# Block-sorted attention and a gated MLP on one core: first batch's V by transfers, and a new order of units

## The chip, the cores and the metric

The kernel runs on one core of a Trainium2 chip. The metric is the device time of one execution in microseconds; lower is better. Times of several runs are given as a median with the lowest and the highest.

## The reference

Four batches, eight heads, 768 tokens, head size 64; the tokens of a head stand in 8 blocks of 96. A 8x8 matrix P per head is normalised five times (exponential, rows, columns); K and V are mixed over blocks with it; attention runs inside each block; the result goes through a gated MLP whose gate mixes tokens.

```python
P = sort_net
for _ in range(5):
    P = P - np.max(P, axis=-1, keepdims=True)
    P = np.exp(P)
    P = P / (np.sum(P, axis=-1, keepdims=True) + 1e-09)
    P = P / (np.sum(P, axis=-2, keepdims=True) + 1e-09)
k_sorted = np.einsum('bhij,bhjcd->bhicd', P, k_b)      # the same for v
scores = scale * np.matmul(q_b, k_sb.transpose(0, 1, 2, 4, 3))
attn = softmax(scores)                                  # over the keys of the block
x = np.matmul(attn, v_sb)                               # heads side by side: 768 x 512 per batch
h = np.maximum(x @ w_in, 0.0)                           # 512 -> 1024
u, v = h[..., :512], h[..., 512:]
v_s = np.einsum('ts,bsd->btd', w_spatial, layernorm(v)) + b_spatial[None, :, None]
out = (u * v_s) @ w_out
```

## The kernel before

The work is cut into units, each a few instructions on one or two engines, and `ORDER` is a written-out list of the units in the order in which they are issued. Every engine runs its own instructions in that order and waits where an operand isn't ready, so the list decides what stands behind a wait. A unit is `NAME:arguments`; where the first argument is a digit it is one of four PSUM tiles (`ps0` to `ps3`), and a letter A, D or P says that ScalarE (ACT), VectorE (DVE) or GpSimd (POOL) takes the result out.

Loads: `L:q:b:lo:hi`, `L:k`, `L:v` (heads lo to hi of batch b, cast to bf16 by the transfer, issued by POOL, 768 KB as it lands), `L:wu`, `L:wv` (the halves of w_in, 512 KB), `L:wsa`, `L:wsb` (the halves of w_spatial, 576 KB), `L:wo`, `BI` (the bias). `LH` loads half of the first batch's q uncast by a hardware queue, and `QC` casts it. `S0` loads the sort matrix, `SK:n` is one of the five normalisations (an exponential on ACT, six small operations on DVE), `PR`, `P0`, `PC`, `PD` spread the result into block-mixing matrices `pd`, for batch 0 by DVE and for the others by POOL. `DM` are dummy matmuls that keep TensorE (PE) busy before there is work.

Attention of a batch, by pairs of heads `hp` (0 to 3) and halves of blocks `ih` (0, 1): `QT` turns q on PE (12 transposes, L314), `QQ` does two pairs. `KT` mixes and turns K in one step (12 matmuls, L383, into `kt_all`). `SC` makes scores (8 matmuls, L442) and their exponential on ACT (L447) into one of 5 buffers `ex_all`. `AT` multiplies by V (8 matmuls, L488), and DVE divides by the sums (L495, L496). V must stand with its keys on partitions, as `vb`, one buffer for even and one for odd batches. Batches 1 to 3: `VM` mixes V whole, 2 matmuls of 128x384 for a pair of heads (L410), into `vm`; `VC:b:lo:hi` copies `vm` into `vb` block by block with one 99 KB transfer for each of 8 blocks, issued by SP (L423). Batch 0: `VT` mixes V as K is mixed (12 matmuls, L383) and `VB` turns it back (8 transposes, L401).

The MLP: `XT`, `XX`, `XD` turn the attention's output (on PE by 2 pairs or by 4, or by a transfer), `VP` (one or two of 6 token tiles, L554) and `UP` (L597) are the first layer, `WW` turns w_spatial (L531), `ST`, `LN`, `LA` normalise, `SP` mixes tokens (L609), `GT` multiplies the gate, `OP`, `OE`, `OS` are the last layer with its copies and stores. `SH`, `GH`, `OH`, `OI`, `OJ` do the same for the end of batch 3 in smaller pieces. `QP` and `QX` turn the last batch's q by a transfer. `IV:n` sets the columns of ones in `vb[0]`, `vb[1]` or `vm` (n = 2) on POOL.

Work of several batches is interleaved, and all four batches use the same four PSUM tiles.

Of the kernel before, what the change touches and what calls it, by code (L numbers as in the profile page):

```python
# [28 lines left out]
UP:1:A:0:0:1 LA:0:2 AT:0:1:1:1 LA:0:3 LA:0:1 LA:0:0 SC:2:1:2:1 UP:3:A:0:1:1 AT:0:1:2:1 LA:0:4 VM:1:A:2:0 WW:2:D:0
VM:3:A:2:1 LA:0:5 L:k:3:0:8 SC:0:1:1:0 WW:1:D:2 VM:3:A:2:3 XT:2:D:1:1:0 VM:0:D:2:2 SC:1:1:0:0 AT:3:1:3:0 QQ:2:D:2:2  # L30
AT:0:1:1:0 SP:1:0:1 XT:2:A:1:1:2 AT:3:1:0:0 SP:0:0:3 VC:2:4:8 GT:P:0:3 XT:1:A:1:0:2 XT:2:D:1:0:0 SP:3:0:0 KT:1:A:2:2
KT:0:A:2:0 VC:2:0:4 KT:2:D:2:3 QQ:3:A:2:0 KT:1:A:2:1 SC:2:2:2:1 VP:0:A:1:0:1 GT:D:0:0 QP:A:3:3 ST:1:1 ST:1:0
VP:3:A:1:4:5 ST:1:4 ST:1:5 GT:P:0:1 SC:1:2:0:0 SC:2:2:1:1 SP:0:0:2 SC:3:2:0:1 SC:1:2:3:1 VP:2:A:1:2:3 QP:A:3:1
GT:D:0:2 AT:1:2:0:0 UP:3:A:1:0:1 ST:1:2 AT:0:2:3:1 UP:2:A:1:0:0 ST:1:3 LN:1:0:6 AT:3:2:1:1 LA:1:3 OP:0:0:0:2 OE:A:0:0
LA:1:5 AT:3:2:0:1 VM:1:A:3:2 QP:A:3:2 UP:2:A:1:1:0 QP:D:3:0 LA:1:2 LA:1:1 VM:3:D:3:0 OP:0:0:2:2 QX:3:0:4 LA:1:0
AT:1:2:2:1 OE:A:0:2 KT:3:A:3:1 KT:2:D:3:2 LA:1:4 XD:2:1 SC:1:2:2:0 SC:0:2:1:0 SC:3:2:3:0 OP:2:0:4:2 VM:0:D:3:1
AT:3:2:2:0 SP:1:1:3 OE:A:0:4 AT:0:2:1:0 AT:2:2:3:0 SP:3:1:2 UP:1:A:1:1:1 KT:2:D:3:3 GT:D:1:2 XD:2:0 KT:0:A:3:0
VM:3:A:3:3 VC:3:4:8 SP:1:1:1 SC:2:3:1:1 SC:0:3:2:1 VP:3:D:2:4:5 SC:0:3:3:1 SC:2:3:1:0 ST:2:4 OS:0:4 VP:1:A:2:0:1
# [27 lines left out]
def kernel(  # L66
# [58 lines left out]
    nc.scalar.preload_act_table_set("natural_log_exp_and_others")  # L125
# [104 lines left out]
    def u_SK(n, safe=False):  # L230
# [13 lines left out]
        nc.vector.reduce_sum(out=cols, in_=p_all.rearrange("p i j -> p j i"), axis=AX.X)
# [151 lines left out]
    def u_VB(ps, eng, b, hp):  # L396
        b, hp = int(b), int(hp)
        t = ps_tile(ps, BF16)[0:BLK, 0, :].rearrange("p (i c) -> p i c", i=NB)
        vT = turned("vT", b, hp)
        for i in range(NB):  # L400
            nc.tensor.transpose(t[:, i, :], vT[:, i * BLK:(i + 1) * BLK], ident)  # L401
# [18 lines left out]
    def u_VC(b, lo, hi):  # L420
        b = int(b)
        for i in range(int(lo), int(hi)):
            queue("S").dma_start(  # L423
                out=vb[b % 2][:, i].rearrange("c h d -> c (h d)"),
                in_=vm[i * TB:(i + 1) * TB].rearrange("t g h d -> t g (h d)"),
            )
# [400 lines left out]
```

## Time and profile before

| | us |
|---|---|
| median of 3 runs | 156.18 (155.99 to 156.47) |
| span of the profiled execution, first to last instruction | 154.5 |
| PE busy in it | 146.7 |
| DVE busy | 115.4 |
| ACT busy | 85.5 |
| POOL busy | 39.4 |

The profile gives the profiled execution its span alone; the median of the timed runs is 1.7 us above that span. Starts in the trace count from the start of the span. In a row of a group stand the line, the engine, the operation, the tiles written and read, the shape and the count; then the busy time in us, the mean of one instruction in ns, and the engine's idle time before them. The chain of work is followed back from the last instruction, each piece with its start, its length in us, its engine and line. Rows of transfers give the size and the time from the start of the issue to the landing.

### The profile page before, as it was taken

To read this page: it belongs to the slowest core of one execution; us is meant where nothing else is said; L and a number is where in the kernel's file an instruction comes from. 1 tells how busy PE (TensorE), PEld (TensorE's weight loads), DVE (VectorE), ACT (ScalarE), POOL (GpSimd) and SP (SyncE) were. 2 spreads that over 40 slices of the span, in tenths; PEclk is the share of its full clock that TensorE was granted. 3 is DMA by queue.
4 is the path that set the end of the run, shared out by engine and by line. 5 is a ranking of instruction groups with operands and counts; after the bars stand their busy time and mean duration, and the time that the engine had idled before them with its cause. 6 is when DMAs were issued, how large, how long until landed. Compare 5 with 4: busy or idle time off the path is not lost.

```text
span 154.5 us, 4033 instructions
## 1 busy us (share of the span) xinstructions
PE 146.7 (95%) x1689; PEld 95.7 (62%) x1689; DVE 115.4 (75%) x258; ACT 85.5 (55%) x116; POOL 39.4 (25%) x45
## 2 busy tenths in 40 slices
...
DMA  2999999999999999990069358704708400307756
GB/s 68 270 204 203 204 206 204 209 216 248 223 205 256 205 231 245 208 195 15 4 118 125 67 102 167 182 3 37 205 0 215 163 0 4 132 4 284 268 191 220
DMA packets 30693, 24.36 MB, mean 158 GB/s; under 512 B 10384, under 2 KB 27792, under 8 KB 30672
## 3 DMA queue, kind: packets, MB, share of 16 engines
...
q10 hardware_dynamic: 576, 0.66, 1.2%
...
## 4 chain that ended last, share of the span: by engine, by line
PE 84%; DMA 7%; ACT 2%; DVE 2%; POOL 1%; issue 1%; POOLq 0%; ACTq 0%
PE ps L609 15%; PE ps L554 14%; PE ps L597 14%; PE ps L635 10%; DMA k_in<-in_k_dram 7%; PE ps L442 5%; PE ps L488 5%; PE ps L665 5%; PE ps L383 4%; PE ps L685 3%; PE ps L314 2%; PE ps L410 2%; PE ps L518 2%; ACT ex_all L447 2%; PE ps L531 1%; PE ps L401 1%
## 5 line engine op out<-in xcount | busy, mean ns | idle before, releaser
L626 POOL TENSOR_TENSOR gt<-z,u_sb 128x768 bf16<-128x768 f32 x7 | 11.4, 1640 | 77.0 <-DVE z L615 47.6
L447 ACT ACTIVATE ex_all<-ps 96x768 bf16<-96x768 f32 x32 | 24.7, 806 | 5.7 <-PE ps L442 5.5
L609 PE MATMUL ps<-wspT,v_sb 128*128 128x384 bf16 x144 | 25.1, 326 | 0.0
L597 PE MATMUL ps<-xT,w_in_sb 128*128 128x384 bf16 x128 | 22.8, 326 | 0.0
L496 DVE TENSOR_TENSOR x_sb<-ps,rec_all 96x512 bf16<-96x512 f32 x32 | 22.0, 686 | 1.1
L554 PE MATMUL ps<-w_in_sb,xT 128*128 128x512 bf16 x96 | 22.3, 380 | 0.0
L571 DVE BATCH_NORM_STATS2 stats<-v_sb 128x6 f32<-128x512 bf16 x24 | 16.3, 678 | 4.5 <-ACT v_sb L121 4.5
L115 ACT COPY o_sb<-ps 128x1024 f32<-128x1024 f32 (+1 forms) x12 | 10.9, 905 | 14.6 <-PE ps L685 9.1
L609 PEld LDWEIGHTS <-v_sb 128*128 128x128 bf16 x144 | 13.6, 97 | 8.6
L121 ACT ACTIVATE v_sb<-ps 128x1024 bf16<-128x1024 f32 (+1 forms) x11 | 10.3, 948 | 12.3 <-PE ps L554 12.3
L615 DVE TENSOR_TENSOR z<-ps,b_bc 128x768 f32<-128x768 f32 x12 | 11.4, 954 | 7.3 <-PE ps L609 4.6
L635 PE MATMUL ps<-w_out_sb,gt 128*128 128x256 bf16 x144 | 16.9, 273 | 0.0
L121 ACT ACTIVATE u_sb<-ps 128x768 bf16<-128x768 f32 x12 | 9.7, 811 | 12.7 <-PE ps L597 12.7
L597 PEld LDWEIGHTS <-w_in_sb 128*128 128x128 bf16 x128 | 11.8, 97 | 7.2
L635 PEld LDWEIGHTS <-gt 128*128 128x128 bf16 x144 | 13.8, 97 | 2.1
L554 PEld LDWEIGHTS <-xT 128*128 128x128 bf16 x96 | 8.7, 97 | 9.9
L488 PEld LDWEIGHTS <-ex_all 96*128 96x128 bf16 x256 | 10.7, 97 | 4.0 <-issue 0.5
L488 PE MATMUL ps<-vb,ex_all 96*128 96x65 bf16 x256 | 12.6, 193 | 0.5 <-ACT ex_all L447 0.5
L226 PE MATMUL ps<-warm 128*128 128x512 bf16 x36 | 9.5, 425 | 1.3 <-DVE warm L201 1.3
L442 PE MATMUL ps<-qT,kt_all 64*128 64x96 bf16 x256 | 9.8, 205 | 0.9 <-issue 0.4
L115 ACT CAST kt_all<-ps 128x768 bf16<-128x768 f32 x11 | 8.7, 801 | 2.2 <-PE ps L383 2.2
L442 PEld LDWEIGHTS <-kt_all 64*128 64x128 bf16 x256 | 6.4, 94 | 5.5 <-issue 3.3
...
## 6 DMA issues: line engine op xcount, KB each, us to landing
...
v_in<-in_v_dram POOLq DMA_DIRECT2D x4, 768.0 KB, 21.4
k_in<-in_k_dram POOLq DMA_DIRECT2D x4, 768.0 KB, 23.7
...
q_in<-in_q_dram POOLq DMA_DIRECT2D x3, 768.0 KB, 28.2
...
q<-in_q_dram SPq DMA_DIRECT2D x1, 768.0 KB, 4.6
```

The costliest lines, as they stand in the source:

```text
L115: nc.scalar.copy(out=out, in_=in_)
L121: nc.scalar.activation(out=out, in_=in_, func=AF.Relu)
L442: nc.tensor.matmul(t[:, hh, 0:HW].rearrange("p (g x) -> p g x", g=G)[:, :, ii * TB:(ii + 1) * TB], lhsT=kT[rows, i * BLK:i * BLK + 128], r ...
L447: nc.scalar.activation(out=e_tile(b, hp, ih).rearrange("p h (x g) -> p h x g", g=G), in_=t[0:BLK, :, 0:HW].rearrange("p h (g x) -> p h x g ...
L488: nc.tensor.matmul(t[:, hh, ii * VW:ii * VW + D + 1], lhsT=e[:, c:c + 128], rhs=vb[b % 2][:, ih * NI + ii, 2 * hp + hh, 0:D + 1], start=Tr ...
L496: nc.vector.tensor_mul(out=x_sb[:, hp].rearrange("p i (h d) -> p h i d", h=2), in0=tv[:, :, :, 0:D], in1=_raw_ap(rec, 0, [rec.ap[0], [NI, ...
L554: nc.tensor.matmul(t[:, x, :], lhsT=st["xT", b][:, n // 3, kc, (n % 3) * 128:(n % 3 + 1) * 128], rhs=w_in_sb[:, kc, DH:DFF], start=(kc == ...
L571: nc.vector.bn_stats(out=stats, in_=st["v_sb", b, n])
L597: nc.tensor.matmul(t[:, x, 0:HW], lhsT=w_in_sb[:, kc, mc * 128:(mc + 1) * 128], rhs=st["xT", b][:, ih, kc, :], start=(kc == 0), stop=(kc = ...
L609: nc.tensor.matmul(t[:, x, 0:HW], lhsT=st["v_sb", b, n][:, mc * 128:(mc + 1) * 128], rhs=wspT[:, 3 * x:3 * x + 3, n, :], start=(n == 0), s ...
L615: nc.vector.tensor_add(out=z.rearrange("p (x c) -> p x c", x=2), in0=t[:, :, 0:HW], in1=b_bc.rearrange("p (x c) -> p x c", x=2),)
L635: nc.tensor.matmul(t[:, x, c:c + w], lhsT=st["gt", b, mc][:, (n0 + x) * 128:(n0 + x + 1) * 128], rhs=w_out_sb[:, mc, c:c + w], start=(mc = ...
```

## The change

1. Batch 0's V takes the way of the other batches: four `VM:..:0:..` and `VC:0:..` in place of four `VT` and four `VB`. `VC` gets an argument for the queue, and two of the eight groups of transfers (`VC:0:4:8:0:4:A` and `VC:2:0:4:0:4:A`, four transfers each) are issued by ScalarE.
2. All units have a new order. The loads come as v0, half of q0, k0, q1, v1, k1, wu, wv, wsa, wsb, v2, bias, k2, q2, q3, v3, wo, k3; before, as v0, k0, half of q0, v1, q1, k1, wv, wsb, wu, v2, wsa, q2, bias, k2, q3, wo, v3, k3 (digits are batches).
3. `LH:A` issues the first batch's half of q from ScalarE's queue, ahead of the load of its table (`TB`, which was the first instruction).
4. `SK` writes P a second time by columns (`p_cols`), so that the column sums read neighbours and the two multiplications have the strided side.
5. `vT` gets a zero margin, `vt_all`, and `VB` whole 128-row transposes; neither the new order nor the fall-back path behind `IF` issues a `VT` or a `VB` any more.
6. Several copies change their engine; some store transfers are issued by ScalarE.

```diff
 ORDER = """
-S0 CO SK:0 BH LH:S:0 IV:2 L:v:0:0:8 SK:1 SK:2 ID MA L:k:0:0:8 L:q:0:4:8 DM:3:6:512 DM:0:6:512 L:v:1:0:8 L:q:1:0:8
-QC:A:0 SK:3 QC:A:1 MB SK:4 DM:2:6:512 DM:1:6:512 MC QT:2:D:0:1 DM:1:6:512 DM:3:6:512 PR:1 L:k:1:0:8 QT:2:A:0:0 P0:0:2
-L:wv L:wsb P0:4:6 P0:6:8 IV:0 P0:2:4 PC:D VT:0:A:0:0 KT:3:D:0:0 L:wu PD:1:0:4 VT:2:A:0:1 L:v:2:0:8 KT:1:A:0:3
-KT:0:D:0:2 SC:2:0:0:1 VB:3:D:0:0 PD:1:4:8 KT:1:A:0:1 QT:0:D:0:2 IV:1 QT:2:A:0:3 VB:3:D:0:1 SC:0:0:1:0 VT:1:D:0:3
-VT:2:A:0:2 L:wsa L:q:2:0:8 SC:3:0:0:0 PD:3:0:4 PD:3:4:8 BI AT:0:0:0:1 L:k:2:0:8 VB:1:D:0:3 SC:2:0:1:1 AT:3:0:0:0
-VM:0:A:1:0 VB:1:D:0:2 SC:2:0:2:0 AT:3:0:1:0 SC:0:0:3:0 AT:1:0:2:0 SC:2:0:2:1 AT:3:0:1:1 VM:0:A:1:2 AT:2:0:3:0
-XT:1:A:0:0:0 VM:0:D:1:3 QQ:3:D:1:2 SC:1:0:3:1 VM:2:D:1:1 XT:0:A:0:1:0 KT:1:A:1:2 L:q:3:0:8 AT:3:0:3:1 VC:1:4:8
-KT:0:A:1:1 AT:2:0:2:1 KT:1:A:1:0 VC:1:0:4 QQ:3:D:1:0 KT:0:A:1:3 PD:2:0:4 XT:2:D:0:0:2 XT:1:D:0:1:2 PD:2:4:8 L:wo
-SC:3:1:0:1 SC:0:1:2:0 VP:2:D:0:0:1 ST:0:0 SC:0:1:1:1 SC:1:1:3:1 ST:0:1 VP:3:A:0:4:5 VP:2:A:0:2 VP:1:A:0:3 ST:0:5
+L:v:0:0:8 L:q:0:4:8 S0 LH:A:0 TB CO SK:0 BH ID SK:1 SK:2 MA IV:2 DM:3:6:512 DM:0:6:512 QC:A:0 SK:3 QC:A:1 MB SK:4
+L:k:0:0:8 DM:2:6:512 DM:1:6:512 MC DM:1:6:512 L:q:1:0:8 DM:3:6:512 QT:0:D:0:0 PR:1 P0:0:2 VM:2:A:0:0 P0:2:4 P0:4:6
+P0:6:8 PC:A VM:3:D:0:1 VM:0:A:0:2 VM:2:A:0:3 VC:0:4:8:0:4:A QT:1:D:0:1 PD:1:0:4 QT:3:D:0:2 KT:0:D:0:1 PD:1:4:8
+KT:1:A:0:0 KT:2:D:0:3 L:v:1:0:8 QT:3:D:0:3 KT:0:D:0:2 SC:2:0:1:1 SC:1:0:0:1 L:k:1:0:8 SC:3:0:3:1 QQ:2:D:1:0 QT:0:D:1:2
+QT:1:D:1:3 SC:3:0:2:1 L:wu SC:2:0:1:0 AT:0:0:1:1 VC:0:0:4 SC:1:0:2:0 AT:3:0:0:1 AT:2:0:2:1 SC:0:0:0:0 L:wv VM:1:A:1:1
+L:wsa XT:3:D:0:1:0 PD:2:0:4 AT:0:0:3:1 SC:2:0:3:0 VM:3:A:1:3 AT:1:0:0:0 VM:0:A:1:0 AT:2:0:1:0 VM:3:A:1:2 AT:1:0:3:0
+KT:0:A:1:0 AT:2:0:2:0 KT:3:A:1:2 KT:1:D:1:3 KT:0:A:1:1 XT:2:D:0:1:2 XX:3:D:0:0 SC:1:1:3:1 SC:0:1:1:1 UP:2:A:0:0:1
+SC:3:1:0:1 PD:2:4:8 SC:1:1:2:1 VP:0:A:0:1 VP:2:A:0:0 L:wsb VP:3:A:0:4:3 ST:0:1 VC:1:4:8 AT:1:1:0:1 L:v:2:0:8
+AT:0:1:3:1 BI IV:1 VP:2:D:0:5:2 SC:3:1:3:0 SC:1:1:2:0 UP:0:A:0:1:1 L:k:2:0:8 AT:3:1:1:1 L:q:2:0:8 AT:2:1:2:1 WW:1:A:0
+WW:0:D:2 ST:0:5 UP:3:A:0:1:0 XT:2:D:1:1:2 ST:0:0 L:q:3:0:8 XT:1:A:1:1:0 WW:0:A:4 ST:0:3 SC:3:1:1:0 ST:0:4 ST:0:2
+SC:2:1:0:0 LN:0:0:6 VC:1:0:4 UP:1:A:0:0:0 UP:0:A:1:1:1 VM:3:D:2:0 LA:0:2 UP:2:A:1:0:1 LA:0:1 LA:0:3 LA:0:5 PD:3:4:8
+VM:1:A:2:1 LA:0:4 VP:3:A:1:4 VP:0:A:1:3 LA:0:0 AT:2:1:0:0 KT:1:A:2:1 QQ:3:D:2:2 PD:3:0:4 KT:0:A:2:2 KT:2:D:2:0
+L:v:3:0:8 QQ:1:A:2:0 QP:A:3:2 KT:3:D:2:3 VM:0:A:2:2 QP:D:3:1 SP:2:0:2 AT:3:1:2:0 L:wo AT:1:1:1:0 SP:0:0:0 AT:2:1:3:0
...
-    nc.scalar.preload_act_table_set("natural_log_exp_and_others")
+    def u_TB():
+        nc.scalar.preload_act_table_set("natural_log_exp_and_others")
...
+    p_cols = const.tile([BH, NB, NB], FP32, name="p_cols")
...
-        nc.vector.tensor_mul(out=p_all, in0=p_all, in1=over_rows(rowsum))
-        nc.vector.reduce_sum(out=cols, in_=p_all.rearrange("p i j -> p j i"), axis=AX.X)
+        nc.vector.tensor_mul(out=p_cols.rearrange("p j i -> p i j"), in0=p_all, in1=over_rows(rowsum))
+        nc.vector.reduce_sum(out=cols, in_=p_cols, axis=AX.X)
...
-        nc.vector.tensor_mul(out=to, in0=p_all, in1=over_cols(colsum))
+        nc.vector.tensor_mul(out=to, in0=p_cols.rearrange("p j i -> p i j"), in1=over_cols(colsum))
...
-    def u_VC(b, lo, hi):
-        b = int(b)
+    def u_VC(b, lo, hi, h0=0, h1=HP, eng="S"):
+        b, heads = int(b), slice(2 * int(h0), 2 * int(h1))
         for i in range(int(lo), int(hi)):
-            queue("S").dma_start(
-                out=vb[b % 2][:, i].rearrange("c h d -> c (h d)"),
-                in_=vm[i * TB:(i + 1) * TB].rearrange("t g h d -> t g (h d)"),
+            queue(eng).dma_start(
+                out=vb[b % 2][:, i, heads].rearrange("c h d -> c (h d)"),
+                in_=vm[i * TB:(i + 1) * TB, :, heads].rearrange("t g h d -> t g (h d)"),
             )
```

More of the change, by code (lines that the diff above doesn't have):

```diff
@@ L29 @@
[L29 to L38, printed above, removed]
@@ new lines @@
+VM:3:A:2:3 GT:P:0:0 SP:1:0:3 QP:P:3:3 VC:2:0:4:0:4:A XX:0:D:1:0 SC:3:2:3:0 ST:1:4 SC:2:2:2:1 L:k:3:0:8 VC:2:4:8
+SP:1:0:1 SC:3:2:0:0 SC:0:2:2:0 GT:D:0:2 ST:1:3 VP:2:A:1:2:0 AT:1:2:3:0 GT:P:0:3 GT:P:0:1 QP:D:3:0 AT:3:2:2:1
+VP:0:D:1:1:5 ST:1:2 SC:2:2:0:1 SC:1:2:1:0 OP:3:0:0:2 VM:2:A:3:0 OE:D:0:0 AT:0:2:0:0 UP:1:A:1:1:0 AT:2:2:1:0 AT:3:2:2:0
+ST:1:5 QX:3:0:4 UP:0:A:1:0:0 SC:1:2:3:1 SC:2:2:1:1 OP:3:0:4:2 ST:1:0 ST:1:1 LN:1:0:6 OE:A:0:4 VM:0:D:3:3 LA:1:5
+VM:1:D:3:1 OP:2:0:2:2 LA:1:3 XD:2:0 AT:0:2:0:1 OE:A:0:2 VM:3:A:3:2 VP:1:A:2:1:0 LA:1:0 AT:2:2:1:1 VP:0:D:2:2 OS:0:2
@@ new lines @@
+LA:1:4 LA:1:2 LA:1:1 VC:3:0:4 KT:3:A:3:2 KT:1:A:3:1 KT:2:D:3:3 KT:0:A:3:0 UP:3:D:2:1:0 VC:3:4:8 ST:2:2 SP:1:1:1
+AT:2:2:3:1 SP:0:1:0 SC:3:3:3:0 SC:1:3:1:0 GT:P:1:0 ST:2:1 SP:2:1:2 AT:0:3:3:0 AT:3:3:1:0 XD:2:1 SP:1:1:3 GT:P:1:2
+UP:2:D:2:1:1 ST:2:0 SC:0:3:1:1 SC:3:3:2:0 VP:1:A:2:4 AT:2:3:1:1 GT:D:1:3 VP:0:D:2:3 SC:3:3:3:1 SC:1:3:0:0 UP:2:D:2:0:1
+VP:3:A:2:5 SC:0:3:2:1 ST:2:4 ST:2:5 SC:1:3:0:1 GT:P:1:1 ST:2:3 OP:2:1:2:2 OE:A:1:2 AT:3:3:2:1 AT:0:3:2:0 LN:2:0:6
+LA:2:5 OP:1:1:4:2 LA:2:3 AT:2:3:3:1 LA:2:0 OS:0:0:0:2:A AT:3:3:0:0 LA:2:2 UP:0:A:2:0:0 LA:2:4 LA:2:1 OP:2:1:0:2
@@ L46 @@
+AT:3:3:0:1 XD:3:0 OE:D:1:0 SP:0:2:0 SP:3:2:2 IV:0 GT:P:2:2 OE:A:1:4 OS:1:0:0:2:A SP:1:2:3 XD:3:1 GT:D:2:0 VP:2:D:3:4:5
+SP:0:2:1 ST:3:5 CK VP:3:D:3:2:1 UP:1:A:3:1:0 ST:3:1 VP:2:A:3:3 VP:0:A:3:0 GT:P:2:1 GT:P:2:3 OS:0:4 ST:3:2 ST:3:0
+ST:3:4 OP:1:2:2:2 ST:3:3 CF:2 LF LN:3:0:6 LA:3:5 UP:3:D:3:0:0 OP:0:2:0:2 LA:3:0 LA:3:4 OE:A:2:0 OE:D:2:2 OS:1:2
+OP:2:2:4:2 LA:3:3 OE:A:2:4 UP:0:A:3:0:1 LA:3:1 LA:3:2 UP:3:A:3:1:1 SH:0:3:2:0 SH:3:3:3:0 GH:P:3:3:0 SH:2:3:0:0
 GH:D:3:2:0 SH:0:3:1:0 GH:P:3:0:0 SH:3:3:1:1 SH:2:3:2:1 OS:2:4 GH:P:3:1:0 SH:1:3:3:1 OS:2:0 GH:D:3:1:1 SH:3:3:0:1
@@ L153 @@
     kt_all = const.tile([128, NK, S + 32], BF16, name="kt_all")
+    vt_all = const.tile([128, 2, S + 32], BF16, name="vt_all")
     ex = [ex_all[:, n] for n in range(NE)]
@@ L157 @@
     st = {}
-    count = {"e": 0, "k": 0}
+    count = {"e": 0, "k": 0, "v": 0}
     def ld_tile(name):
```

18 lines of the change are left out of this document (6 added, 12 removed).

## The prediction

> **What bounds the kernel now.** I read the page first, then the chain of waits in order of time, then the groups of instructions, then the transfers one by one.
>
> ```profile
> span 154.5 us, 4033 instructions
> PE 146.7 (95%) x1689; PEld 95.7 (62%) x1689; DVE 115.4 (75%) x258; ACT 85.5 (55%) x116; POOL 39.4 (25%) x45
> ...
> DMA  2999999999999999990069358704708400307756
> ```
>
> PE is busy nearly throughout, but the last row shows a second full resource: the transfer engines are at 9 from the second slice to the eighteenth, about 4 to 69 us. The chain tells where each of the two rules.
>
> ```profile
> 2.88 10.96 DMA k_in<-in_k_dram
> ...
> 18.54 0.79 PE ps L383 x24
> ...
> 20.16 0.36 PE ps L488 x8
> ...
> 33.13 1.83 PE ps L554 x8
> ...
> 38.97 0.70 PE ps L531 x12
> 39.67 0.28 PE ps L442 x8
> ...
> 40.30 1.30 PE ps L597 x8
> 41.60 0.24 PE ps L488 x8
> ...
> 46.85 0.33 PE ps L410 x2
> ...
> 49.55 0.34 PE ps L518 x8
> ...
> 54.65 1.95 PE ps L609 x12
> ...
> 79.40 0.21 DVE rec_all L495
> 79.64 0.70 DVE x_sb L496
> ...
> 145.89 5.21 PE ps L685 x32
> ```
>
> The chain begins with the load of the first K, which lands at 13.84. The first multiplication with V (`AT`, L488) is at 20.16, the first MLP matmul (`VP`, L554) at 33.13; from there PE is the chain until 151.10, except for 1.0 us at 79.4, where it waits for DVE (the two rows of `AT`'s division, with the gaps around them). So 33.13 to 151.10, 118.0 us, is PE's own work; before 33.13 it is a mixture, and time can be won or lost there without PE's sum telling it. After 151.10 come 3.4 us of last copies and stores, which the change leaves alone.
>
> **A mark that both orders share.** By the order, the new kernel's first MLP unit is `UP:2:A:0:0:1`. At it the same units are done as in the old one at its first `VP`: all attention of batch 0, its `XT`s, V, K and Q of batch 1, two of batch 1's scores. What PE still has to do is the same set of matmuls in another order. Call the time of that first MLP matmul U: the end moves by U - 33.1, and by the waits after it, against 1.0 us of waits in the old order.
>
> **Part by part, ahead of the mark.**
>
> ```profile
> L383 PE MATMUL ps<-pd,v_in 128*64 128x128 bf16 x48 | 1.9, 220 | 0.1
> L401 PE MATMUL ps<-ident,vT 128*96 128x128 bf16 x32 | 2.5, 222 | 0.1
> L410 PE MATMUL ps<-v_in,pd 128*128 128x384 bf16 x24 | 5.9, 326 | 0.0
> ...
> L447 ACT ACTIVATE ex_all<-ps 96x768 bf16<-96x768 f32 x32 | 24.7, 806 | 5.7 <-PE ps L442 5.5
> L115 ACT CAST vm<-ps 128x768 bf16<-128x768 f32 x7 | 5.6, 799 | 0.1
> L117 DVE CAST kt_all<-ps 128x768 bf16<-128x768 f32 x5 | 4.8, 955 | 1.3 <-PE ps L383 1.2
> L495 DVE RECIPROCAL rec_all<-ps 96x8 f32<-96x8 f32 x32 | 6.2, 193 | 3.7 <-PE ps L488 3.5
> L496 DVE TENSOR_TENSOR x_sb<-ps,rec_all 96x512 bf16<-96x512 f32 x32 | 22.0, 686 | 1.1
> L117 DVE COPY xT<-ps 128x768 bf16<-128x768 bf16 x4 | 2.1, 547 | 0.0
> L244 DVE TENSOR_REDUCE colsum<-p_all 32x8 f32<-32x64 f32 x4 | 1.0, 256 | 0.1
> L239 DVE TENSOR_REDUCE rowsum<-p_all 32x8 f32<-32x64 f32 x4 | 0.8, 207 | 0.9 <-ACT p_all L238 0.9
> ...
> ```
>
> `VT` and `VB` give back 1.9 + 2.5 = 4.4 us of PE; four `VM` of two matmuls cost a third of L410's 5.9, 2.0 us. PE is 2.4 us lighter (2.7 by the chain's pitches), all of it ahead of the mark, where PE waits for others.
>
> P by columns: five column sums go from a strided 256 ns to something like the contiguous 207, -0.2 us. Ten multiplications get a strided side; the trace has none, so 0 to the same 49 ns each, up to +0.5. Sum -0.2 to +0.3; I take 0, since both are small against fixed costs. The table load now stands behind the issue of `LH`:
>
> ```profile
> 0.82 1.28 ACT L125 ACT_TABLE_LOAD   x1 [0.82 <-PEq L811]
> ...
> 1.21 0.42 SPq L348 DMA_DIRECT2D q<-in_q_dram  x1
> ...
> 12.30 1.41 DVE L270 TENSOR_TENSOR pd<-mask,ps 128x256 bf16<-128x256 bf16 x4 [0.39 <-PE ps L256]
> ```
>
> 0.82 + 0.42 + 1.28 = 2.52 against 2.10; the first exponential also waits for the sort matrix, so `pd` starts 0 to 0.4 us after 12.30, and I take 12.4. Then the first `VM` ends at 13.2; ACT copies three results of 0.80 and `PC` of a third the width (I take 0.4), 2.8 us, and is done near 16.2. DVE's one (0.955 behind `pd`, which ends near 13.8) is earlier. So batch 0's `VC` starts at 16.2.
>
> ```profile
> L423 SPq DMA_DIRECT2D vb<-vm x24: 572/596/1092, 29.6 to 98.0; - x24
> ...
> DMA to landing us min/median/max: 2.7/5.8/7.0
> ```
>
> Four transfers go out from ACT's queue and four from SP's, at 0.6 us each; the fourth starts at 18.0. A landing takes 2.7 (transfer engines idle) to 7.0 us (full). They are full here, and eight come in 2.4 us instead of 4.8, so I take 6: V is there at 24.0 (20.7 to 25.0), and the first `AT` runs at 24 instead of 20.16. ACT pays 2.4 us of issuing, in front of one K copy and all exponentials; five of those at 0.81 end near 23.4, so this is covered by V's landing, and costs up to 2 us if that cover goes.
>
> From the first `AT` DVE is the row: eight divisions at 0.193 + 0.686 = 0.88, two `XT` copies of 0.55 and one K copy of 0.955 stand before the first `UP` can read `xT`: 7.0 + 1.1 + 0.95 = 9.1, from 24.3 to 33.4. So U = 33.4, within 32.3 (below) and 34.4 (V at 25.0). The 2.4 us of PE are handed to the transfer of V.
>
> **The loads after the mark.**
>
> ```profile
> 1.29 1.06 POOL L171 DMA_DIRECT2D v_in<-in_v_dram  x1 [0.36 <-issue]
> ...
> 5.39 0.90 POOL L171 DMA_DIRECT2D q_in<-in_q_dram  x1
> 6.25 0.91 POOL L171 DMA_DIRECT2D k_in<-in_k_dram  x1
> ...
> 20.64 0.92 POOL L171 DMA_DIRECT2D q_in<-in_q_dram  x1 [2.50 <-PE ps L488]
> ```
> ```profile
> q_in<-in_q_dram POOLq DMA_DIRECT2D x1, 768.0 KB, 18.5
> ```
> ```profile
> k_in<-in_k_dram POOLq DMA_DIRECT2D x1, 768.0 KB, 21.5
> ```
> ```profile
> q_in<-in_q_dram POOLq DMA_DIRECT2D x1, 768.0 KB, 28.5
> ```
>
> Issue plus landing: q1 at 23.9, k1 at 27.75, q2 at 49.1. So 768 KB take 3.85 us. Between k1 and q2 land wv, wsb, wu, v2, wsa and q2, 3712 KB, which at that rate is 18.6 us; it took 21.4. The other 2.8 us are batch 1's `VC`, the only other traffic: one batch of `VC` costs the load stream 2.8 us. That is the price of the new `VC` of batch 0, and the page's DMA row says that nothing is free to hide it.
>
> In the new order k1 has the same loads before it, so 27.75 + 2.8 less 0.3 (v0's issue no longer stands behind a memset): 30.2; wu 32.8, wv 35.4. U can hardly be before wu: 32.8, or 32.3 if `VC` delays it by less. k0 has q's half ahead of it, 13.84 + 1.9 - 0.3 = 15.4, no bound, as V comes later. q2 now also has k2 (3.85) and the bias (384 KB, at most 1.9, I take 0.9) ahead: 49.1 + 2.8 + 3.85 + 0.9 - 0.3 = 56.3; q3 follows 3.85 later, 60.2.
>
> Its reader is `QQ:3:D:2:2`. Between U and it PE has 6 `UP` (1.30), 8 tiles of `VP` (1.83 / 2 = 0.915), 6 `SC` (0.28), 5 `AT` (0.24), 3 `WW` (0.70), 2 `XT` (0.34), 2 `VM` (0.33), a `KT` (0.40): 7.8 + 7.3 + 1.7 + 1.2 + 2.1 + 0.7 + 0.7 + 0.4 = 21.9, so PE is there at 55.3 and waits 1.0 for q2. Behind it `QP:A:3:2` on ACT waits for q3, and behind that the copy of `VM:0:A:2:2`, whose PSUM tile `SP:0:0:0` needs: 60.2 + 0.8 + 0.8 = 61.8. Up to there PE has two `QQ` (24 transposes each, 0.8 as the 24 matmuls of the L383 row), three `KT`, a `VM`, an `SP` (1.95) and two `AT`, 5.6 us, so from 56.3 it comes at 61.9 and needn't wait a second time. So 1.0 us in all, as much as the old 1.0.
>
> POOL's queue: the ones for `vb[1]` (`IV:1`) wait for batch 1's first two `AT` and for a `VC`, near U + 6 = 39, and k2, q2 and q3 stand behind it. Issued ahead of it are w_in, w_spatial, v2 and the bias, which keep the stream full until 30.2 + 10.9 (2176 KB) + 3.85 + 0.9 = 45.9, so this cover holds by some 6 us; without it each us of `IV:1` would be one of q2. ACT's other four `VC` (2.4 us, near 64) delay two exponentials with 2.0 us of `SP` to hide them. At the end DVE gets the flag test, five tiles' statistics and two copies that were ACT's in a row, ahead of the last `LA` that `SH` reads: nothing, as PE still has three `UP` of 1.30 and three `OP` there, to one such copy's 0.955 us; with no row nearer to either, I take 0.5.
>
> **The sum.** Span: 33.4 + 118.0 - 1.0 + 1.0 + 0.5 = 151.9 for PE's last matmul against 151.10, +0.8; span 155.3. The median of the runs, 156.18, lies 1.7 above this profile's span, which I leave as it is: 157.0.
>
> [...]
>
> **Rivals.**
> *Faster: V and the loads come early.* If the two queues get V in at once (landing 2.7, the shortest in that row) and the loads lose little by it, V is there at 20.7, U is set by wu at 32.3, q2 comes at 56.3 - 2.8 = 53.5, where PE is at 54.2, and no wait is left: 32.3 + 117.0 + 0.5 = 149.8, -1.3, 154.9. For it: the first slices of the DMA row are not full, so the loads may be ahead by more than the 0.3 us that I gave them. Against it: the 2.8 us measured for the same transfers. [...]
>
> *Slower: ScalarE becomes the bound ahead of the mark.* Its 2.4 us of issuing come when the scores are ready. From 16.2 to the last K copy ahead of the first `UP` ACT has that, eight exponentials, four V copies and four K copies, 2.4 + 6.5 + 3.2 + 3.2 = 15.3 us, to 31.5 without a gap; its exponentials and copies wait for PE in turn, and with 3.5 us of gaps the last K copy and not DVE sets U, at 35. PE ends at 35 + 117.0 + 1.0 (0.5 as above and 0.5 of exponentials still behind) = 153.0, as PE no longer waits for q2: +1.9, 158.1. It decides from 1.9 us of gaps on, where ACT passes DVE's 33.4.
>
> *No effect.* The head could come out with U + waits equal to the old within 0.4 us, since every term is a wait that shifts with its neighbour: 156.2.
>
> **How the numbers follow.** The forecast, V and loads as summed, 0.45; faster rival 0.28; slower rival 0.17; no effect 0.10. About 0.3%, 0.5 us, is what a measurement of this kernel can tell from no change. Faster by more: the rival's 0.28 and 0.05 of the forecast's lower side, 0.33. Slower by more: 0.17 and 0.33 of the forecast's 0.45, whose middle is +0.8, 0.50. Within: the other 0.07 of the forecast and no effect, 0.17. The range reaches from the faster rival's 154.9 less the 0.5 for DVE at the end, 154.4, to the slower rival's 158.1 plus the other 0.5 that DVE can take there, 158.6.
>
> **What would show it.** Right: the first `AT` near 24, waiting for `vb`; U at 33 to 34; `QQ` or the copies behind q3 waiting for a load at 55 to 62; k1's landing near 30 and q2's near 56. Wrong: an `AT` at 21, U below 32.5, or q2 before 54.

## The result and the profile after

The changed kernel takes 168.29 us (median of 4 runs, 166.78 to 171.21) against 156.2 us (155.99 to 156.47); the ratio is 1.0749, 95% interval 1.0721 to 1.0777. The forecast was 157.0 (154.4 to 158.6): the sign was right, the size was not. The profiled run took 168.14 us. Comparisons leave disturbed runs out, and where a time below stands without a ratio (two of the experiments), the runs of that kernel lay too far apart for one; a part of that spread is explained below.

The page of the changed kernel, its head, the clock and transfer rows of its slices, and the shares of its chain:

```profile
span 166.3 us, 3904 instructions
PE 148.6 (89%) x1611; PEld 96.9 (58%) x1617; DVE 119.2 (72%) x264; ACT 76.0 (46%) x108; POOL 43.1 (26%) x47
...
PEclk9997598799999999999599999999999999999999
DMA  4999999999999999499534193400248200309236
...
PE 62%; DMA 14%; DVE 10%; ACT 5%; ACTq 3%; issue 2%; SPq 1%; DVEq 0%
```

The span grew by 11.8 us and PE's busy time by only 1.9, so PE now waits. The chain says for what: 14% of the span is `DMA`, and its own table of lines gives all of that to `vb<-vm`, the copy of V into key order. The clock row is new too: 7, 5, 9, 8 and 7 in the slices between 12 and 33 us and a 5 near 80, where the old kernel's clock stood at 1.00 in each of these stretches. The first slow stretch, from 14 to 21 us, stands behind no long wait (PE was busy 2.6 of the 4 us from 10 to 14, with no gap above 0.92), and it costs nothing, as PE came to the first `AT` at 24.24, before V. The chain in order of time (start, length, engine and line):

```profile
16.13 0.70 ACTq L428
...
17.51 1.01 ACTq L428
18.54 8.97 DMA vb<-vm
28.22 0.99 PE ps L493 x16
29.65 0.75 PE ps L415 x2
...
36.69 7.27 DMA vb<-vm
...
67.90 0.81 ACT vm L115
...
71.16 7.30 DMA vb<-vm
78.51 0.55 PE ps L493 x13
79.06 3.21 PE ps L559 x8
...
132.90 0.96 DVE z L620
...
140.89 0.59 DVE stats L576
141.90 0.55 issue
142.45 1.46 PE ps L602 x8
143.91 3.49 PE ps L640 x32
```

The three long `DMA` pieces are the copies of V of batches 0, 1 and 2, and near the end nine microseconds of DVE lead to a PE instruction that follows 0.55 us after them. What PE itself saw is in its timeline (in brackets the idle time before a row and what ended it):

```profile
24.24 0.22 PE L493 MATMUL ps<-vb,ex_all 96*128 96x65 bf16 x2
26.64 0.19 PE L493 MATMUL ps<-vb,ex_all 96*128 96x65 bf16 x1 [2.18 <-DMA vb<-vm]
27.56 0.31 PE L493 MATMUL ps<-vb,ex_all 96*128 96x65 bf16 x5 [0.73 <-DMA vb<-vm]
...
37.61 1.47 PE L602 MATMUL ps<-xT,w_in_sb 128*128 128x384 bf16 x8
...
44.00 0.55 PE L493 MATMUL ps<-vb,ex_all 96*128 96x65 bf16 x13 [0.81 <-DMA vb<-vm]
...
77.75 0.19 PE L493 MATMUL ps<-vb,ex_all 96*128 96x65 bf16 x1 [2.21 <-DMA vb<-vm]
78.51 0.55 PE L493 MATMUL ps<-vb,ex_all 96*128 96x65 bf16 x13 [0.56 <-DMA vb<-vm]
...
142.45 1.46 PE L602 MATMUL ps<-xT,w_in_sb 128*128 128x384 bf16 x8 [3.06 <-DVE flag L732]
```

From these rows the account: the first MLP matmul, the prediction's mark U, is at 37.61 instead of 33.13, +4.5. Behind it come waits that the old order has not: 0.8 for batch 1's V, 2.8 for batch 2's, 3.1 for a flag. In the chain, the `VP` behind batch 2's V takes 3.21 us against the 1.83 that eight such matmuls took in the old chain, +1.4. Together 12.6. Against that, the old kernel's PE stood idle 0.3 us behind U, and apart from the slow row the new order keeps PE busy 0.8 us less there (118.3 us with the 1.4 in it, against 117.7): 11.5 of the 11.9 by which PE's last matmul moved, from 151.1 to 163.0. The rest lies in gaps of under 0.25 us.

The flag: `CK` and `CF` test on DVE and PE whether a denominator has left its bounds, and `LF` reads the answer into a register of every engine that takes the branch behind it. In the old order two `UP` and more stand between `CF` and `LF`; in the new one `LF` stands directly behind `CF`, whose last step on DVE waits in DVE's queue behind five tiles' statistics. So PE's own queue stops at `LF`, matmuls that do not need the flag included, here for the 3.06 us of the timeline.

### The profile page after: what moved, and what is told of

The parts are those of the page before. It is cut to its first block, busy times and chain, and to the rows that moved or that the text cites. A ratio compares the mean times of both kernels' runs of the same rounds, so it can differ in the third digit from the quotient of the medians.

```text
span 166.3 us, 3904 instructions
## 1 busy us (share of the span) xinstructions
PE 148.6 (89%) x1611; PEld 96.9 (58%) x1617; DVE 119.2 (72%) x264; ACT 76.0 (46%) x108; POOL 43.1 (26%) x47
## 4 chain that ended last, share of the span: by engine, by line
PE 62%; DMA 14%; DVE 10%; ACT 5%; ACTq 3%; issue 2%; SPq 1%; DVEq 0%
DMA vb<-vm 14%; PE ps L614 12%; PE ps L602 11%; PE ps L640 9%; PE ps L559 8%; PE ps L670 5%; PE ps L493 5%; PE ps L690 3%; ACT vm L115 3%; PE ps L447 3%; ACTq L428 3%; PE ps L415 2%; DVE stats L576 2%; PE ps L388 2%; PE ps L536 1%
## 5 line engine op out<-in xcount | busy, mean ns | idle before, releaser
L452 ACT ACTIVATE ex_all<-ps 96x768 bf16<-96x768 f32 x32 | 24.1, 805 | 27.9 <-PE ps L447 24.6
L631 POOL TENSOR_TENSOR gt<-z,u_sb 128x768 bf16<-128x768 f32 x9 | 15.3, 1714 | 69.6 <-ACT ex_all L452 28.2
L559 PE MATMUL ps<-w_in_sb,xT 128*128 128x512 bf16 x90 | 24.0, 399 | 0.5
L576 DVE BATCH_NORM_STATS2 stats<-v_sb 128x6 f32<-128x512 bf16 x24 | 16.2, 673 | 3.7 <-ACT v_sb L121 3.6
L602 PEld LDWEIGHTS <-w_in_sb 128*128 128x128 bf16 x128 | 11.8, 98 | 10.5 <-issue 3.1
L493 PEld LDWEIGHTS <-ex_all 96*128 96x128 bf16 x256 | 11.5, 100 | 10.0 <-issue 7.0
L620 DVE TENSOR_TENSOR z<-ps,b_bc 128x768 f32<-128x768 f32 x12 | 11.5, 955 | 5.9 <-PE ps L614 5.8
L559 PEld LDWEIGHTS <-xT 128*128 128x128 bf16 x96 | 9.2, 100 | 10.2 <-issue 1.4
L500 DVE RECIPROCAL rec_all<-ps 96x8 f32<-96x8 f32 x32 | 6.3, 198 | 10.8 <-PE ps L493 10.7
L115 ACT COPY o_sb<-ps 128x1024 f32<-128x1024 f32 (+1 forms) x9 | 7.8, 867 | 13.6 <-PE ps L690 9.3
L115 ACT CAST vm<-ps 128x768 bf16<-128x768 f32 x12 | 9.3, 804 | 6.5 <-PE ps L415 6.5
L683 POOL TENSOR_TENSOR gt<-z,u_sb 128x512 bf16<-128x512 f32 (+1 forms) x5 | 5.2, 1062 | 17.8 <-DVE z L676 17.7
L588 DVE TENSOR_SCALAR v_sb<-v_sb,mv,rstd 128x512 bf16<-128x512 bf16 x24 | 8.6, 404 | 1.2 <-ACT rstd L583 1.2
## 6 DMA issues: line engine op xcount, KB each, us to landing
v_in<-in_v_dram POOLq DMA_DIRECT2D x4, 768.0 KB, 14.7
```

What stands on the lines that cost most here:

```text
L115: nc.scalar.copy(out=out, in_=in_)
L452: nc.scalar.activation(out=e_tile(b, hp, ih).rearrange("p h (x g) -> p h x g", g=G), in_=t[0:BLK, :, 0:HW].rearrange("p h (g x) -> p h x g ...
L493: nc.tensor.matmul(t[:, hh, ii * VW:ii * VW + D + 1], lhsT=e[:, c:c + 128], rhs=vb[b % 2][:, ih * NI + ii, 2 * hp + hh, 0:D + 1], start=Tr ...
L559: nc.tensor.matmul(t[:, x, :], lhsT=st["xT", b][:, n // 3, kc, (n % 3) * 128:(n % 3 + 1) * 128], rhs=w_in_sb[:, kc, DH:DFF], start=(kc == ...
L576: nc.vector.bn_stats(out=stats, in_=st["v_sb", b, n])
L602: nc.tensor.matmul(t[:, x, 0:HW], lhsT=w_in_sb[:, kc, mc * 128:(mc + 1) * 128], rhs=st["xT", b][:, ih, kc, :], start=(kc == 0), stop=(kc = ...
```

## Experiments

The theory after the two traces: four losses that add, V's late landing at the start, batch 2's V, the flag, and PE's clock behind long waits; V is late because its transfers share the engines with the loads. The rivals: that a repaired wait only uncovers the next one; that the new order itself, not V, makes the start late; that V is late by its issue and length and not by the loads.

Each ratio is against runs of the old kernel beside it, whose median lay at 156.0 to 156.2.

**The flag read later** (e1_flag_late).

```
- CF:2 LF LN:3:0:6 ...  UP:3:A:3:1:1 SH:0:3:2:0
+ CF:2 LN:3:0:6 ...     UP:3:A:3:1:1 LF SH:0:3:2:0
```

> The changed kernel with one unit moved: the reading of the branch flag by all engines (LF) stands behind the last UP of batch 3 instead of right behind the flag's matmul. Theory (the flag): in the changed kernel TensorE sits idle from 139.4 to 142.45 us because it must read a flag that VectorE makes only behind five tiles' statistics; with the reading behind three UP and two OP, those run in that time, and the end comes 2.6 to 3.1 us earlier, 165.0 to 165.7 against 168.3. Rival (VectorE is the bound at the end, the flag only marks it): the last LA still comes at the same time behind statistics and copies, SH waits for it, and the gain is under 1 us.

165.36 us (164.52 to 165.98), ratio 1.0579 (1.0544 to 1.0613): 2.9 less than the changed kernel. PE's list of waits has no flag row any more, and the waits for V sum to as much as before:

```profile
PE ps L493 <- DMA vb<-vm: 6.4, 5, 2.5
PE ps L230 <- DVE warm L204: 1.3, 1, 1.3
PE ps L447 <- ACT kt_all L115: 1.0, 1, 1.0
```

From U to its last matmul PE takes 121.3 us in this trace instead of 125.4: 3.1 of the 4.1 are the flag, most of the rest is batch 1's V, for which PE didn't wait here. U itself came 1.9 us later than in the changed kernel's trace (39.52), with batch 0's V landing at 28.4. The flag's 3.1 us are shown: a unit of no arithmetic at all, put too early.

**The old order, V by transfers** (e3_old_order_transfers): of the change only its first point.

```
- VT:0:A:0:0 .. VT:2:A:0:1 .. VT:1:D:0:3 VT:2:A:0:2  VB:3:D:0:0 VB:3:D:0:1 VB:1:D:0:3 VB:1:D:0:2
+ VM:0:A:0:0 VM:2:A:0:1 VM:1:D:0:2 VM:0:A:0:3 VC:0:0:4 VC:0:4:8    (behind PC)
```

> The kernel before, in its own order, with part 1 alone: VM in place of batch 0's VT, all four right behind the mixing matrices, eight VC from SyncE's queue, no VB. Theory (V's landing): the copies start near 16 us and the last half lands at 25 to 27, so the first AT moves from 20.2 to 25 or later and the first MLP matmul from 33.1 to 37 or 38: 160 to 162 us, without any new order. Rival (the order alone is at fault, the transfers are as good as the turning): within 0.7 us of 156.2, as TensorE has 2.4 us less to do.

165.43 us (165.3 to 165.73), ratio 1.0599 (1.0581 to 1.0616): worse than either theory. The timeline of PE, and the windows (busy time of PE, PEld, DVE, ACT, POOL, then the granted clock):

```profile
25.20 0.21 PE L488 MATMUL ps<-vb,ex_all 96*128 96x65 bf16 x1 [5.46 <-DMA vb<-vm]
...
27.32 0.44 PE L488 MATMUL ps<-vb,ex_all 96*128 96x65 bf16 x5 [0.56 <-DMA vb<-vm]
```
```profile
20.00:22.00 2.00, 0.00 (x0) 0.00 (x0) 0.00 (x0) 1.15 (x2) 0.86 (x1) 1.00 1.25 237
22.00:24.00 2.00, 0.00 (x0) 0.00 (x0) 0.00 (x0) 0.00 (x0) 1.98 (x3) 0.95 1.24 246
...
32.00:36.00 4.00, 4.00 (x52) 2.90 (x50) 3.27 (x7) 2.41 (x3) 0.00 (x0) 0.50 1.19 209
```

V is there at 27.32 instead of 20.16, 7.2 us of the loss, and after a wait of 5.5 us PE's clock is at half, 0.50 in each window from 24 to 36 us, though PE is busy again. U comes at 42.45, and behind it PE takes 118.0 us as before, so the whole loss lies ahead of U: the other 2.2 us are in the stretch from V to U, 15.1 us instead of 12.9. The transfers alone, put into the old order, cost 9.4 us: it has no other work for the wait.

**The old order with dummy matmuls in the wait** (e7_old_order_warm).

```
- BI AT:0:0:0:1
+ BI DM:1:24:512 AT:0:0:0:1
```

> The old order with batch 0's V by transfers (165.4 us, 9.2 above the old kernel), and now 24 dummy matmuls in PE's 5.5 us wait for V. Clock theory: of the 9.2 us, V's landing is only about 5, and the rest is PE at half clock from 24 to 37 us, because it stood idle from 19.7 to 25.2. Kept busy, it keeps its clock, the first MLP matmul comes at 38 to 39 instead of 42.5, and the time falls by 3.5 to 6 us, to 159.5 to 162. Rival (V's landing and the loads behind it set the start, clock or not): less than 1 us below 165.4.

165.69 us (165.02 to 166.36), ratio 1.0621 (1.0582 to 1.0659): no gain, my expectation missed. The clock was 1.00 from 20 to 24, while the dummies ran, and still from 24 to 28, when PE was busy 1.93 of the 4 us; the drop came afterwards, to 0.67 and 0.50:

```profile
24.00:28.00 4.00, 1.93 (x27) 1.00 (x24) 0.52 (x2) 0.28 (x1) 0.62 (x1) 1.00 1.27 233
28.00:32.00 4.00, 3.25 (x52) 2.29 (x51) 2.77 (x7) 3.05 (x5) 0.89 (x1) 0.67 1.27 210
32.00:36.00 4.00, 4.00 (x52) 2.87 (x51) 2.92 (x6) 2.16 (x3) 0.00 (x0) 0.50 1.17 205
```

So this run does not tell what the clock costs in the old order.

**The new order, V turned twice** (e2_new_order_turned): the rest of the change without its first point; `VT` and `VB` taken out by ACT and DVE at places of my choice, and `IV:0` moved to the front.

```
- VM:2:A:0:0 ... VM:3:D:0:1 VM:0:A:0:2 VM:2:A:0:3 VC:0:4:8:0:4:A ... VC:0:0:4
+ VT:2:A:0:0 ... VT:3:D:0:1 VB:0:A:0:0 VB:2:A:0:1 VT:0:A:0:2 VT:3:D:0:3 VB:2:A:0:2 VB:3:A:0:3
```

> The changed kernel and its order with part 1 undone: batch 0's V is again mixed by VT and turned back by VB (results taken out by ScalarE, which no longer issues transfers there), the VC of batch 0 are gone; everything else stays. Theory (V's landing): the first AT comes near 21 to 22 us instead of 27.6, the first UP at 33 to 35 instead of 37.6, and the stretch of low TensorE clock behind the wait goes: 163.0 to 165.0 us. The waits for batch 2's V and for the flag stay. Rival (the order's loads set the first UP, whichever way V goes): the first UP stays at 36 or later, at most 1.5 us faster, 166.8 or more.

166.83 us (165.93 to 168.27), ratio 1.0704 (1.0636 to 1.0772), nearer to the rival, the order itself: the first `AT` at 26.72, U at 36.13. The new order puts other work ahead of the first `AT`, so it cannot use a V that is early; but where `VT`'s and `VB`'s copies stand was my choice, so this is no clean measure of the order, and how much of the late start is the order's own stays open. An estimate: in the traces of the changed kernel, e1, e5 and e11 PE came to the first `AT` at 23.4 to 24.5, and with the 9.4 us from V to U that e8 shows, a V in time would give U at 32.8 to 33.9, about the old 33.1; no run shows it. The flag's 3.1 and batch 2's 2.4 are there as in the changed kernel.

**Batch 2's V earlier** (e5_batch2_early): its last `VM` ahead of three `AT` and an `SP`, its eight `VC` from SP right behind, and two of the `AT` in the other order.

```
- SP:2:0:2 AT:3:1:2:0 L:wo AT:1:1:1:0 SP:0:0:0 AT:2:1:3:0 VM:3:A:2:3 GT:P:0:0 ... VC:2:0:4:0:4:A ... VC:2:4:8
+ SP:2:0:2 VM:3:A:2:3 VC:2:0:4 VC:2:4:8 AT:1:1:1:0 L:wo AT:3:1:2:0 SP:0:0:0 AT:2:1:3:0 GT:P:0:0
```

> The changed kernel with batch 2's last VM two units earlier and its eight VC right behind it, all from SyncE's queue, instead of four from ScalarE's queue 4.6 us of TensorE's work later and four from SyncE's. Theory (each batch's V lands too late for its reader): the wait of 2.8 us at 75.5 to 78.5 goes, and with it the half clock behind it that makes eight VP matmuls take 3.2 instead of 1.8 us: 4 us less, 163.8 to 165.0. Rival (the wait only moves to the next load or to ScalarE): under 1.5 us less.

165.54 us (164.86 to 167.15), ratio 1.0624 (1.0555 to 1.0693): 2.8 less, between the 4 of the theory and the rival's 1.5. PE's waits:

```profile
PE ps L602 <- DVE flag L732: 3.1, 1, 3.1
PE ps L493 <- DMA vb<-vm: 2.4, 3, 1.1
PE ps L447 <- ACT kt_all L115: 1.7, 1, 1.7
```

The wait for V fell from 6.5 to 2.4: the 2.8 of batch 2 are gone, and the other 1.4 is batch 0's V, which this edit doesn't touch (it landed at 26.35 here, and U came 1.2 earlier). The 1.7 behind a K copy on ACT end at 20.69, ahead of the first `AT`, where PE would have waited for V in any case. What took back a part is the flag, still in place: behind the same wait these two rows now take 2.9 us longer than the 1.46 and 3.49 that they take in the changed kernel (by 2.72 against 1.46, about half clock, an estimate). The chain of e5:

```profile
137.15 2.72 PE ps L602 x8
...
139.87 5.16 PE ps L640 x32
```

**Loads held until V has landed** (e9_loads_held): q1 and every load behind it stand in POOL's queue behind `IV:0`, moved here from a later place, which waits for V's transfers.

```
- DM:1:6:512 L:q:1:0:8 DM:3:6:512 ... VC:0:4:8:0:4:A ... PD:1:4:8 KT:1:A:0:0 ... VC:0:0:4
+ DM:1:6:512 DM:3:6:512 ... VC:0:4:8:0:4:A VC:0:0:4 ... PD:1:4:8 IV:0 L:q:1:0:8 KT:1:A:0:0
```

> The new kernel, with the loads of q1, v1 and k1 held back until all eight transfers of batch 0's V have landed, so that V goes alone over the transfer engines. Contention theory: V lands at 20 to 21 instead of 27.5 and the first multiplication with V runs at 21 to 22.5; the three loads are then some 5 us later, so the first MLP matmul is at 36 to 38 and the time within 1.5 us of 168.3. Rival (V is late because of its issue and its own length, not because of the loads): the first multiplication with V waits for V until 25 or later.

174.61 us (171.63 to 176.6). The landing times of the `VC` from 14 us on (to 45 in the changed kernel, first block; to 40 here, second block), and PE's longest wait here:

```profile
DMA to landing us min/median/max: 5.2/6.8/9.1
```
```profile
DMA to landing us min/median/max: 2.9/3.3/3.6
```
```profile
PE ps L319 <- DMA q_in<-in_q_dram: 9.0, 1, 9.0
```

The same 99 KB transfers land in 3.3 us alone and in up to 9.1 beside the loads: contention it is. V was there by 22.7, when `IV:0` behind it ran. But q1 was then loaded alone and late, and PE waited 9.0 us for it; U came at 43.49. I had expected 36 to 38 for U and a time within 1.5 us of 168.3, and the fastest of the four runs, 171.63, lies 1.8 us above that: q1, the first of the held loads, was issued at 23.14 and landed 7.2 us later, and I had not put it on PE's path.

**Only v1 and k1 held** (e10_k1_v1_held).

```
- PD:1:4:8 KT:1:A:0:0 ... L:v:1:0:8 ... VC:0:0:4
+ (VC:0:0:4 behind VC:0:4:8:0:4:A)  PD:1:4:8 IV:0 KT:1:A:0:0 ... L:v:1:0:8
```

> The new kernel with v1 and k1 (and the loads behind them) held until batch 0's V has landed, q1 left where it was. Contention theory: with only q1 beside it, V is there between the 22.6 of all loads held and the 27.5 of none, at 24 to 26; but v1 then lands near 30, k1 near 34 and the first half of w_in near 37, so that the first MLP matmul is at 37 to 39 and the time 168 to 170: what V gains the loads lose. Rival (the loads have slack at this place): the first MLP matmul at V plus 9.4, 33.5 to 35.5, time 165 to 166.5.

171.08 us (169.49 to 173.48), ratio 1.0919 (1.0872 to 1.0967). V was there by 22.61, earlier than I had expected (24 to 26), with landings of 3.8 to 4.9 us beside q1 alone, though from two queues. The first `AT` ran at 23.62 without a wait for V, and PE waited for v1 instead:

```profile
PE ps L415 <- DMA v_in<-in_v_dram: 4.7, 1, 4.7
```

U 38.99, as expected; what V gains, the loads lose, and somewhat more.

**V from one queue** (e11_one_queue).

```
- VC:0:4:8:0:4:A
+ VC:0:4:8
```

> The new kernel with all eight transfers of batch 0's V issued by SP, as for the other batches. Contention theory (the landing is long because the casting loads fill the transfer engines): the eight issues end near 21 instead of 19.7, the last landing is 6 to 7.5 us behind, 27 to 28.5 against 27.5, and the time is within 1 us of 168.3. Rival (two queues in flight at once are what stretches a landing to 9 us): V there at 25 or earlier, time 2 us or more lower.

168.63 us (167.76 to 170.72), ratio 1.0773 (1.0748 to 1.0798). PE's timeline, and the clock behind it:

```profile
25.03 0.31 PE L493 MATMUL ps<-vb,ex_all 96*128 96x65 bf16 x5 [0.94 <-DMA vb<-vm]
...
36.81 1.48 PE L602 MATMUL ps<-xT,w_in_sb 128*128 128x384 bf16 x8
```
```profile
28.00:30.00 2.00, 2.00 (x26) 1.56 (x24) 0.67 (x2) 0.80 (x1) 0.00 (x0) 0.50 1.32 205
```

Half of each theory. The time is the same, but V was there at 25.03, where the rival had it. The first `AT` reads blocks 4 to 7. One queue sends those first, and they land by 24.98 (by 25.32 in e12), the other four in e12 by 28.33. Two queues send the others beside them, and the eight land mixed (in the changed kernel ACT's four at about 21.4 to 27.5, SP's at 21.7 to 27.7): the last of the four that are waited for came at 27.52 in the changed kernel, at 28.39 in e1 and at 26.35 in e5. The 2.5 us so won did not reach the end. PE ran at half clock behind the wait (0.50 from 28 to 32 us), so that U came only 0.8 earlier, and behind the flag's wait the `UP` and `OP` took 1.99 and 4.64 us, 1.7 more than in the changed kernel's trace.

**Dummies in four waits** (e6_warm).

```
- QT:0:D:0:0 PR:1 ... VM:2:A:0:3 VC:0:4:8:0:4:A ... QT:3:D:0:2 KT:0:D:0:1 ... AT:0:0:1:1
+ QT:0:D:0:0 DM:3:5:512 PR:1 ... VM:2:A:0:3 DM:3:6:512 VC:0:4:8:0:4:A ... QT:3:D:0:2 DM:0:4:512 KT:0:D:0:1 ... DM:0:14:512 AT:0:0:1:1
```

> The new kernel with dummy matmuls put into four of PE's waits ahead of the first MLP matmul (the longest row of them directly before the first multiplication with V). Nothing else moves. Clock theory: of the 4.5 us by which the first MLP matmul is late, a part is not V's landing but matmuls at a lower granted clock behind the wait (0.73 between 27.6 and 34 us). With PE kept busy the clock stays at 1.0 there, the first MLP matmul comes at 35 to 36.5 instead of 37.6, and the time falls by 1.0 to 2.5 us from 168.3, to 165.8 to 167.3. Rival (PE only waits; what runs slowly at a low clock is hidden behind DVE's row of divisions): within 0.7 us of 168.3, whatever the clock shows.

170.73 us (167.78 to 171.19); no gain, and none in the fastest run either (the changed kernel's is 166.78). The clock was 1.00 in every window to 80 us, and U came 9.3 us behind V instead of 10.0; but with the dummies V's transfers began 0.6 us later (16.75) and V came at 28.59, and U stayed at 37.89. Its profile shows one reason why runs of one kernel differ by some us: PE's timeline at the flag, and the chain behind it,

```profile
143.50 1.46 PE L603 MATMUL ps<-xT,w_in_sb 128*128 128x384 bf16 x8 [3.06 <-DVE flag L733]
```
```profile
144.96 5.16 PE ps L641 x32
```

The same 3.06 us of waiting as in the changed kernel; there the 32 matmuls took 3.49, with the clock at 1.00 from 144 to 148, here 5.16, with the clock at 0.60. Seven traces have this wait, of 3.06 or 3.07 us. In three of them (the changed kernel, e2, e9) the eight matmuls of `UP` and 32 of `OP` behind it take 4.95 us in the chain; in e6, e10 and e11 they take 6.6 and in e5 7.9. So behind a wait of this length the matmuls are slower in one run and not in another. The other reason is V's landing, 26.4 to 28.4 in the profiles of e1, e5 and the changed kernel, which send batch 0's V alike.

**The three repairs together** (e8_all_mended): the edits of e1, e5 and e6.

> The new kernel with three repairs together: the dummy matmuls, the flag read behind the last MLP unit, batch 2's V sent two units earlier by one queue. If the losses are separate and add, the time is 168.3 less 2.9 (flag alone) less 2.8 (batch 2 alone) less 1.0 to 2.5 (dummies), 160.1 to 161.6, still above the old 156.2 by V's landing at the start. Rival (the losses hide one another, each repair uncovers the next wait): above 163.

161.43 us (161.13 to 161.87), ratio 1.0342 (1.0313 to 1.0371), as expected if the losses are separate. U is at 37.30 and PE ends at 156.1: 118.8 us of work and waits behind U, to 118.0 before. What is left is, but for 0.8 us, the start.

**Repairs, one queue, dummies only behind the `VM`** (e12_repairs_one_queue): the edits of e1, e5 and e11, `DM:0:4:512` ahead of `KT:0:D:0:1` and `DM:0:8:512` ahead of the first `AT`.

> The new kernel with the flag read late and batch 2's V two units earlier as in the three repairs together (161.4 us there), all of batch 0's V from SP's queue, and dummy matmuls only where they stand behind the four units that mix V: 4 in the wait for K and 8 directly before the first multiplication with V. If the start is V's landing plus 9.4 us at full clock, V is there at 25, the first MLP matmul at 34.4 to 35.2, and the time is 158.5 to 159.5. Rival (the loads of k1 and of w_in hold the start, or the landing is not better than 27): the first MLP matmul at 36 or later, 160.3 or more.

159.07 us (158.35 to 159.34), ratio 1.0192 (1.0171 to 1.0213). PE's timeline and the page's clock row:

```profile
25.36 0.31 PE L493 MATMUL ps<-vb,ex_all 96*128 96x65 bf16 x5 [0.28 <-DMA vb<-vm]
...
35.01 1.48 PE L602 MATMUL ps<-xT,w_in_sb 128*128 128x384 bf16 x8
```
```profile
PEclk9999999999999999999999999999999999999999
```

U at V plus 9.65, the clock full throughout, 118.2 us behind U (PE busy 116.7 and idle 1.5, where the old kernel has 117.7 and 0.3): the forecast of this run held by its steps. Of the change's 12 us, 9 came back by moving units, by one queue and by twelve dummies. The last 3 are 2.3 in the profiled run, the fastest of the four, and 1.9 of these stand ahead of U, where V's landing ends the wait. No version of the change came under the old kernel.

**P by columns alone, in the old kernel** (e4_columns_alone): point 4 of the change's list and nothing else.

> The old kernel with P written by columns and nothing else. By the instruction times in the new kernel's trace (multiplications 0.26 and 0.25 us against 0.21, the column sum 0.21 against 0.26) a pass is 0.05 us longer and five passes 0.25 us; if that is on the path to the first exponential, the time rises by 0.1 to 0.3 us (ratio 1.0006 to 1.002). The forecast's 0 (range -0.2 to +0.3): no difference, or a gain of 0.2.

156.04 us (12 runs) against 156.01, ratio 1.0000 (0.9990 to 1.0009). `pd` started at 12.76 instead of 12.30, and the first MLP matmul came no later (32.78 to 33.08 in the two timelines), probably because the first K lands at 13.84 only.

## Why the prediction was wrong

- **`VC` of batch 0 starts at 16.2**: right, 16.13.
- **V there at 24.0 (20.7 to 25.0)**: wrong, 27.56, the first of the mis-sized terms. I put a landing at 6 us, within the old range of 2.7 to 7.0; the last that the first `AT` reads took 8.97, with eight transfers from two queues beside the loads, and ACT's third issue took 1.0 us instead of 0.6, so that the fourth began at 18.54 and not at 18.0. e9 (3.3 us alone) shows that the loads stretch it, e11 (25.03) that beside the loads the second queue does so for the four that are read first. This landing gives 3.6 of the 4.2 us by which U came behind the forecast's 33.4, the stretch from V to U the rest.
- **DVE's row of 9.1 us from V to U**: nearly right, and in e12 DVE is that row, with one gap above 0.15 us (0.24) from 25.71 to 35.6. V to U is 9.3 in e6, 9.4 in e8 and 9.65 in e12, at full clock (1.00 from 28 to 36 us); 10.0 in the changed kernel and 11.8 in e11, where PE's clock is down (0.58 and 0.50 from 28 to 32 us). The traces show a half rate (0.50) behind waits, and that it differs from run to run: behind the flag's wait of 3.06 us the matmuls were slower in four traces of seven. What sets it off was not shown. The prediction had no term for the clock.
- **118.0 us behind the mark, plus 1.0 for q2 and 0.5 for DVE at the end**: here the larger part of the error lay, 6.9 of 11.1 us (125.4 where the sum had 118.5). The 1.0 us of old waits that the sum takes off is misread, to begin with. The chain goes through DVE's two rows at 79.4, but PE ran K's matmuls beside them and stood idle 0.23 us, as the old kernel's timeline shows:

```profile
79.29 0.86 PE L383 MATMUL ps<-pd,k_in 128*64 128x128 bf16 x24
80.38 0.89 PE L442 MATMUL ps<-qT,kt_all 64*128 64x96 bf16 x24 [0.23 <-DVE x_sb L496]
```

"The same set of matmuls in another order" was true, and e12's 118.2 shows it; that they would wait as little was never worked out for V of batches 1 and 2. For each, the sum would have been last `VM`, copy, 2 us of issue, 6 us of landing, against PE's work up to that batch's `AT`: batch 2 has ACT's copy at 67.90 and the landing at 78.46, and PE was there at 75.3. The text costed those `VC` as ACT's time (two delayed exponentials) and not as the path that they are. 0.8 + 2.8, and 1.4 of clock behind the latter.
- **The end**: the term named the right queue, DVE's, with the flag test and the statistics in it, but not the reader. I looked at who reads the last `LA` and not at who waits for the flag: 3.1 instead of 0.5 (e1).
- **q2 and the loads**: k1 landed at 32.4 (17.75 + 14.7) instead of 30.2 and q2 at 59.5 instead of 56.3, but PE never waited for q2, as it came to `QQ` only at 60.1, 4.8 us later than I had it: the other errors hid this one. Of k1's 2.2 us 1.7 were there at k0 already (17.08 instead of 15.4): v0, the first load, came at 11.3, in the old kernel at 10.0 and in e2 at 9.5, long before any `VC`, and why is open. From k0's landing to k1's are 15.3 us, 14.5 in e12 and 13.7 in e2, which has no `VC` of batch 0: by these traces the copies cost the loads 0.8 to 1.6 us and not 2.8. `IV:1` held POOL's queue to 44.61, within the cover that the prediction gave it. In e12, where PE came to `QQ` 0.2 us after q2, the chain does run through `IV:1`, the loads to q3 and ACT's copies behind it, as the prediction had drawn it, to a PE wait of 0.65 us; e8 has the same 0.65 without q3 in its chain.
- **P by columns at 0**: right in the time. The groups of e4 show +50 ns for the multiplication by rows (262, before 212), +43 for that by columns (255) and -49 for the sum (207, before 256): 0.2 us in five passes, which e4 did not find in the time.
- **The rivals**: V early was refuted by the landing, and even with no loads (e9) it took 2.9 to 3.6 us; ACT as the bound has no trace, since V came after all of ACT's work. What the slower rival lacked was that a transfer, and not an engine, is late three times over.
